# Cosine attention and an MLP mixer on one core: a new order of the end phase, with one product of the weights on GpSimd

## The chip, the cores and the metric

One core of a Trainium2 chip runs the whole program. The metric is the time of one execution in device microseconds; the time before is the median of three runs. The engines are named as in the profile: PE is TensorE's matmul, PEld its weight load, DVE is VectorE, ACT is ScalarE, POOL is GpSimd, SP is SyncE, which issues most DMAs.

## The reference

For 8 batches, 12 heads, 448 positions and heads of 64, attention on normalised rows is followed by a mixer over positions and one over channels:

```python
q_n = q / (np.linalg.norm(q, axis=-1, keepdims=True) + 1e-06)
k_n = k / (np.linalg.norm(k, axis=-1, keepdims=True) + 1e-06)
scores = np.matmul(q_n, k_n.transpose(0, 1, 3, 2)) / tau
attn = softmax(scores)                      # over the last axis
x = (attn @ v), heads side by side          # (8, 448, 768)
h = np.maximum(x.transpose(0, 2, 1) @ w_tok1, 0.0) @ w_tok2     # 448 -> 256 -> 448
u = x + h.transpose(0, 2, 1)
out = u + np.maximum(u @ w_ch1, 0.0) @ w_ch2                    # 768 -> 1536 -> 768
```

## The kernel before, in words

The loop runs over 48 pairs of heads, six to a batch. Each pair is loaded, normalised, transposed, scored, put through the exponential, multiplied by v, and mixed over positions (`tok1`, `tok2`); the result `u` of a batch is transposed into `ut`. The two products of the channel mixer for batches 0 to 5 are cut into units and fed into TensorE's stream beside the attention of later batches. Everything is written out by hand under `manual_schedule`: each engine executes its instructions in the order in which the code names them, and an instruction waits only for the data and buffers that it needs.

The last two batches (B0 and B1, numbers 6 and 7) have no later attention to lie beside. They are computed in an **end phase** (from line 959) that saves matmuls: each of the two channel products is split into 2 x 2 blocks and done with seven half-size products in place of eight, from sums and differences of blocks (Winograd's form of Strassen's method).

*First layer* (`p1` to `p7`, lines 595 to 626). The weights' sums are s1w, s2w, s3 (written in place into `wc1t`) and s4w, made by `fast_weights1`, line 547; the inputs' differences t1x to t4x are made by `fast_x`, line 561. `p1(d)` to `p7(d)` run for d = 0, 1, 2, a third of the hidden channels each; each is one product of 12 matmuls with 448 columns. PSUM banks X, Y and Z are taken in turn from a pool of three (`ps2`). A product that adds onto a bank (`start` is False: p2 on X, p3 on Z, p7 and p4 on Y) waits until the engine that copied out the bank's earlier state is done. The partial results go into SBUF copies: e1 (ScalarE, after p1), e5 (ScalarE, after p5), e16 (VectorE, after p6) and e167 (VectorE, after p7). e16 and e167 have two buffers each, e5 has one. The hidden tile `gt` has four quarters for each d: ScalarE writes the first from p2 with its relu; VectorE adds p3 and e16, then ScalarE takes the relu; VectorE adds p4 and e1; and GpSimd adds e167 and e5 (`c22`, line 616). The relu of the last two, which are the second half of the hidden channels in B0 and in B1, is one operation over both batches (`relus`, line 628).

*Second layer* (`q1` to `q7`, lines 681 to 723). The seven row tiles of 128 rows are tiles 0 to 2 in B0, 4 to 6 in B1, and tile 3, the **shared** tile, with the last 64 rows of B0 and the first 64 of B1. Six form three groups of two (`TILES`, line 644), and each group goes through q1 to q7, 6 matmuls of 384 columns each. The weights' differences t1w to t4w are made by `fast_weights2` (line 635), the differences of the hidden tile s1g to s4g for each group by `fast_g` (line 650, VectorE). Here too q2 adds onto q1's bank (psXo), q3 onto q5's (psZo), q7 and q4 onto q6's (psYo). ScalarE copies q1 to f1 and q5 to f5; VectorE makes f16 and f167 from psYo and f1; VectorE and GpSimd add these to the rows `orow`, which SP stores (`store_row`). The shared tile is multiplied plainly in three column ranges (0 to 384, 384 to 640, 640 to 768; `shared_part`, `shared_out`, `shared_store`). Its first range stands between q1 and the groups, the other two at the end.

The order of the end phase is the list of calls from line 959 to 1045. In it t4x is one GpSimd operation and s4w one VectorE operation (lines 986 and 987), GpSimd then runs t1w, c22(0), t2w, c22(1), c22(2), and the loop of the second layer is:

```python
for g in range(3):
    if g == 2:
        q1(g)
    if g == 0:
        q2(g)
        fast_g(0, 4)
    q5(g)
    q6(g)
    if g == 0:
        fast_weights2(4, nc.vector)
    for n, q in enumerate((q2, q7, q3, q4)):
        if g or n:
            q(g)
        if g < 2:
            fast_g(g + 1, n + 1)
```

Of the kernel before, what the change touches and what calls it, by code (L numbers as in the profile page):

```python
# [7 lines left out]
FP32 = mybir.dt.float32  # L8
FP16 = mybir.dt.float16
AF = mybir.ActivationFunctionType  # L10
# [12 lines left out]
def kernel(  # L23
# [12 lines left out]
    nc = tc.nc  # L36
# [510 lines left out]
    def fast_weights1(n, eng):  # L547
        s, w = fw["s"], w1part
        out, a, b, op = {1: (s[0], w(1, 0), w(1, 1), ALU.add), 2: (s[1], s[0], w(0, 0), ALU.subtract),
                         3: (w(1, 0), w(0, 0), w(1, 0), ALU.subtract), 4: (s[2], w(0, 1), s[1], ALU.subtract)}[n]  # L550
        tt(eng, out if n == 3 else out[:], a[:] if n == 2 else a, b[:] if n == 4 else b, op)
# [9 lines left out]
    def fast_x(k, j0, j1, eng=None):  # L561
        t = fw["t"]
        a, b = {1: (cols(B1, j0, j1), cols(B0, j0, j1)),
                2: (cols(B1, HD + j0, HD + j1), t[1][:, j0:j1]),
                3: (cols(B1, HD + j0, HD + j1), cols(B1, j0, j1)),
                4: (cols(B0, HD + j0, HD + j1), t[2][:, j0:j1])}[k]
        tt(eng or nc.vector, t[k][:, j0:j1], a, b, ALU.subtract)
# [8 lines left out]
    def bank2(kind, d):  # L576
        t = ps2.tile([128, 2, 512], FP32, name=f"ps{kind}_{d}", tag="s")
        {"X": px, "Y": py, "Z": pz}[kind][d] = t
# [9 lines left out]
    def etile(kind, d, bufs=1):  # L588
        e[kind, d] = (tail if kind == "e1" and d == 0 else tail2).tile([128, 2, S], FP32, name=f"{kind}_{d}", tag=kind, bufs=bufs)
        return e[kind, d][:]  # L590
# [12 lines left out]

    def p5(d):
        prod1(5, d, pz, True)
        nc.scalar.activation(out=etile("e5", d), in_=pz[d][:, :, 0:S], func=AF.Copy)

    def p6(d):
        prod1(6, d, py, True)
# [2 lines left out]
    def p7(d):  # L612
        prod1(7, d, py, False)
        tt(nc.vector, etile("e167", d, 2), py[d][:, :, 0:S], e["e1", d][:], ALU.add)

    def c22(d):
        tt(nc.gpsimd, gpart(1, 1, d), e["e167", d][:], e["e5", d][:], ALU.add)

    def p3(d):
        prod1(3, d, pz, False)  # L620
        tt(nc.vector, gpart(0, 1, d), pz[d][:, :, 0:S], e["e16", d][:], ALU.add)
        nc.scalar.activation(out=gpart(0, 1, d), in_=gpart(0, 1, d), func=AF.Relu)

    def p4(d):
        prod1(4, d, py, False)
        tt(nc.vector, gpart(1, 0, d), py[d][:, :, 0:S], e["e1", d][:], ALU.add)

    def relus(d):
        g = gts[B0 // 2][:, HC + 2 * d:HC + 2 * d + 2, :]
        if d == 1:  # L630
            nc.scalar.activation(out=g, in_=g, func=AF.Relu)
        else:
            nc.vector.tensor_scalar_max(out=g, in0=g, scalar1=0.0)

    def fast_weights2(n, eng):
        def w(i, j):
            return wc2t[:, HC * i:HC * (i + 1), DH * j:DH * (j + 1)]

        t = fw["t2"]
        a, b = {1: (w(0, 1), w(0, 0)), 2: (w(1, 1), t[1][:]), 3: (w(1, 1), w(0, 1)), 4: (w(1, 0), t[2][:])}[n]  # L640
        tt(eng, t[n][:], a, b, ALU.subtract)
        fw[2] = {1: w(0, 0), 2: w(1, 0), 3: w(1, 1), 4: t[4], 5: t[1], 6: t[2], 7: t[3]}

    TILES = ((0, 1), (4, 5), (2, 6))
    sg, xo, yo, zo, eo, orow = {}, {}, {}, {}, {}, {}

    def gtile(t, i, j0=0, j1=HC):
# [26 lines left out]
        b, slot = (B0, t) if t < 3 else (B1, t - 3)  # L674
        return u16[b][:, HD * h:HD * (h + 1), slot]

    def etile2(kind, g, bufs=1):
        eo[kind, g] = tail2.tile([128, DH], FP32, name=f"{kind}_{g}", tag=kind, bufs=bufs)
        return eo[kind, g][:]

    def q1(g):
        xo[g] = ps.tile([128, 512], FP32, name=f"psXo_{g}", tag="b")
        prod2(1, g, xo[g][:, 0:DH], True)
        nc.scalar.activation(out=etile2("f1", g, 2), in_=xo[g][:, 0:DH], func=AF.Copy)
        tt(nc.gpsimd, j3(etile2("f1u", g, 2)), j3(eo["f1", g][:]), urow(TILES[g][1], 0), ALU.add)

# [35 lines left out]
        tt(nc.vector, orow[g][1][:, 0:DH], yo[g][:, 0:DH], eo["f1u", g][:], ALU.add)  # L722
        store_row(TILES[g][1], orow[g][1])

    def shared_part(lo, hi, j0, j1):
        if j0 == 0:
            shared[lo] = (ps if lo else ps2).tile([128, 512], FP32, name=f"psF_shared_{lo}", tag="b" if lo else "s")
        psF = shared[lo]
        for j in range(j0, j1):
            for i in range(2):  # L730
                nc.tensor.matmul(psF[:, 0:hi - lo], gts[B0 // 2][:, HC * i + j, 384:512], wc2t[:, HC * i + j, lo:hi],
                                 start=(i + j == 0), stop=(i == 1 and j == HC - 1))

    def shared_out(lo, hi):
        o, psF = shared["o"], shared[lo]
        for r, b, slot in ((0, B0, 3), (64, B1, 0)):
            nc.vector.tensor_tensor(out=j3(o[r:r + 64, lo:hi]), in0=j3(psF[r:r + 64, 0:hi - lo]),
                                    in1=u16[b][r:r + 64, lo // 128:hi // 128, slot], op=ALU.add)
# [27 lines left out]
    with tc.manual_schedule():  # L766
# [142 lines left out]
        for i in range(NPAIR + 1, NP_ALL):  # L909
            b, pj = i // NPAIR, i % NPAIR  # L910
            for c in range(KC):
                score(i, c)
            if i == NPAIR + 1:
                upose(i - 4, 2)
                tok2(i - 2, pe=True)
                pv_wide(i - 1)
                upose_act(i - 2)
                x_wide(i - 1)
                sums(i + 2)
            else:  # L920
                pv_rest(i - 1)
                pv(i - 1, 0)
                pv(i - 1, 1)
            if i == NP_ALL - 1:
                fast_weights1(2, nc.vector)
            if i == NPAIR + 1:
                refill(0)
            elif pj == 2 and 1 < b < B - 1:
                refill(b - 1)
            side(i)  # L930
            if i == NP_ALL - NPAIR:
                fed[1] = (sum(t for t, _ in queue) - fed[0]) / NPAIR
            fed[0] += fed[1]
            unit(True)
            if old(i):
                score(i, KC)
            else:
                score_rest(i)
            if i > NPAIR + 1:
                tok2(i - 2)  # L940
            if i + 1 < DMA_T0:
                tpose(i + 1)
            if due():
                unit(True)
            while due():
                unit()
            tok1(i - 1)
            if i + 3 < NP_ALL:
                sums(i + 3)
            if i == NP_ALL - 3:  # L950
                early.close()
                tail = ctx.enter_context(tc.tile_pool(name="tail", bufs=1, side="right", reuse_waits="tile"))
                tail_tiles()
            if i == NP_ALL - 2:
                fast_weights1(1, nc.gpsimd)
        last = NP_ALL - 1
        while queue:
            unit(True)
# [10 lines left out]
        p2(0)  # L969
        tok2(last - 1, pe=True)  # L970
        tok1(last)
        fast_x(2, 0, 1)
        fast_x(3, 0, 1)
        p2(1)
        upose(last - 1)
        fast_x(2, 1, 2)
        fast_x(3, 1, 2)
        p1(2)
        tok2(last, pe=True)
        bank2("Z", 0)  # L980
# [1 line left out]
        upose(last)  # L982
        p2(2)
        fast_x(2, 2, 3)
        fast_x(3, 2, 3)
        fast_x(4, 0, HD, nc.gpsimd)
        fast_weights1(4, nc.vector)
        fast_weights2(1, nc.gpsimd)
        bank2("Y", 0)
        p6(0)  # L990
        bank2("Y", 1)
# [2 lines left out]
        p7(0)  # L994
        c22(0)
        p7(1)
        fast_weights2(2, nc.gpsimd)
        bank2("Y", 2)
        p6(2)
        p4(0)  # L1000
        p4(1)
        p7(2)
        fast_weights2(3, nc.vector)
        bank2("Z", 1)
        p5(1)
        c22(1)
        bank2("Z", 2)
        p5(2)
        c22(2)
        relus(1)  # L1010
        p4(2)
        p3(1)
        p3(2)
        q1(0)
        relus(0)
        q1(1)
        relus(2)
        shared_part(0, DH, 0, 4)
        fast_g(0, 1)
        shared_part(0, DH, 4, HC)  # L1020
        fast_g(0, 2)
        fast_g(0, 3)
        shared_out(0, DH)
        for g in range(3):
            if g == 2:
                q1(g)
            if g == 0:
                q2(g)
                fast_g(0, 4)
            q5(g)  # L1030
            q6(g)
            if g == 0:
                fast_weights2(4, nc.vector)
            for n, q in enumerate((q2, q7, q3, q4)):
                if g or n:
                    q(g)
                if g < 2:
                    fast_g(g + 1, n + 1)
        for lo, hi in ((DH, D - 128), (D - 128, D)):
            shared_part(lo, hi, 0, HC)  # L1040
            shared_out(lo, hi)
            if lo == DH:
                shared_store(0, hi, (nc.sync, nc.sync))
            else:
                shared_store(lo, hi, (nc.scalar, nc.sync))


# [33 lines left out]
```

## Time and profile before

| what | value |
|---|---|
| median of 3 runs | 388.77 us (387.48 to 388.85) |
| profiled execution, its whole time | 387.23 us |
| its span, from the first to the last instruction | 385.4 us |
| mean granted TensorE clock | 0.995 |
| first product of the end phase, p1(0), starts | 322.32 us |
| first product of the second layer, q1(0), starts | 353.58 us |
| last shared matmuls start | 378.63 us |

Times inside the profile count from the start of the span. A line of the timeline has the start, the time taken, the engine, the line of the kernel, the operation, what it writes and reads with the shapes, how many instructions are merged in it, and in brackets the idle time of the engine just before it and what ended that. The times of matmuls overlap each other by a little, so the pace of a stream is read from start to start. Tiles have the code's names: `e` stands for e1, e5, e16 and e167, `f` for the copies of the second layer, `gt` for the hidden tile.

### The profile page before, as it was taken

What the parts mean: (1) busy time and instruction counts of PE and PEld (TensorE: products, weight loads), DVE (VectorE), ACT (ScalarE), POOL (GpSimd) and SP (SyncE); (2) the same over time, 40 slices, a digit from 0 to 9 for tenths busy, and PEclk for the clock granted to TensorE, in tenths of its full rate; (3) what the DMA queues carried; (4) which work ended last, traced back from release to release, by engine and by line L of the source; (5) the groups of instructions that cost most, each with busy time, mean ns of one, the idle gap of its engine ahead of it and who ended that gap; (6) DMA issues with size and microseconds to landing.
All of it is one profiled execution on the core that took longest, in us unless ns stands there. A gap on an engine that the chain in (4) does not pass through costs nothing.

```text
span 385.4 us, 10254 instructions
## 1 busy us (share of the span) xinstructions
PE 366.6 (95%) x4086; PEld 239.7 (62%) x4086; DVE 253.9 (66%) x563; ACT 230.7 (60%) x395; POOL 276.7 (72%) x403
## 2 busy tenths in 40 slices
PE   7798999999999999999999999999999999896895
PEld 6466666776566666676566666666657766453463
DVE  7789766776346665466437565456437768897973
ACT  6899887855676458746666457746667645415010
POOL 8999988979666586677667587677667880497642
PEclk9899999999999999999999999999999999999999
DMA  7999999989978788879767978868866664000054
GB/s 201 268 245 210 261 247 193 212 163 180 210 182 166 193 178 204 202 134 217 205 148 149 231 158 215 186 139 207 211 153 134 149 126 108 0 0 1 2 162 126
DMA packets 115936, 64.35 MB, mean 167 GB/s; under 512 B 72240, under 2 KB 112304, under 8 KB 115888
## 3 DMA queue, kind: packets, MB, share of 16 engines
q1 hardware_dynamic: 109936, 58.22, 67.0%
q0 software_dynamic: 5616, 5.21, 8.8%
q8 instruction: 32, 0.52, 0.6%
q10 hardware_dynamic: 336, 0.26, 0.2%
q14 instruction: 16, 0.13, 0.1%
HBM read 43.45 MB, written 11.01 MB: 141 GB/s over the span
## 4 chain that ended last, share of the span: by engine, by line
PE 75%; POOL 7%; issue 6%; ACT 5%; DVE 4%; DMA 2%; ACTq 0%; DVEq 0%; POOLq 0%
PE psG L466 21%; PE psF L482 19%; PE psO L383 9%; PE psS L344 8%; PE psU L433 5%; PE psR L419 5%; ACT pt L345 3%; PE psYo L667 2%; PE psQ L351 2%; POOL t1w L536 1%; PE psZo L667 1%; POOL s1w L536 1%; PE psXo L667 1%; PE psO L366 1%; DVE ssq L265 1%
## 5 line engine op out<-in xcount | busy, mean ns | idle before, releaser
L345 ACT ACTIVATE pt<-psS 128x896 f16<-128x896 f32 (+1 forms) x156 | 132.4, 917 | 52.9 <-PE psS L344 52.7
L297 POOL TENSOR_TENSOR kq<-kf,rn 128x384 f16<-128x384 f32 (+1 forms) x47 | 41.9, 891 | 66.7 <-DVE rn L274 62.9
L482 PE MATMUL psF<-wc2t,gt 128*128 128x384 f16 x504 | 88.4, 326 | 0.0
L466 PE MATMUL psG<-ut,wc1t 128*128 128x448 f16 x432 | 88.1, 352 | 0.0
L482 PEld LDWEIGHTS <-gt 128*128 128x128 f16 x504 | 47.1, 98 | 27.8
L466 PEld LDWEIGHTS <-wc1t 128*128 128x128 f16 x432 | 40.2, 98 | 32.4
L469 ACT ACTIVATE gt<-psG 128x448 f16<-128x448 f32 x72 | 38.9, 540 | 33.1 <-PE psG L466 33.1
L265 DVE TENSOR_REDUCE ssq<-sq 128x15 f32<-128x960 f32 (+2 forms) x51 | 56.1, 1100 | 3.3 <-ACT sq L247 3.0
L422 DVE TENSOR_SCALAR rt<-psR 128x256 f16<-128x256 f32 x48 | 20.0, 417 | 50.8 <-PE psR L419 50.8
L297 POOL TENSOR_TENSOR kq<-qf,rn 112x512 f16<-112x512 f32 x45 | 47.1, 1046 | 3.0
L344 PE MATMUL psS<-qk 64*128 64x448 f16 x312 | 41.4, 356 | 3.6 <-DVE qk L323 2.9
L486 DVE TENSOR_TENSOR ost<-psF,u 128x384 f32<-128x384 f32 (+1 forms) x48 | 25.6, 534 | 24.3 <-PE psF L482 22.9
L249 POOL TENSOR_TENSOR sq<-qf 112x512 f32<-112x512 f32 x39 | 40.6, 1042 | 0.0
L249 POOL TENSOR_TENSOR sq<-kf 128x384 f32<-128x384 f32 (+1 forms) x46 | 40.2, 874 | 0.1
L383 PE MATMUL psO<-vt,pt 128*128 128x65 f16 (+1 forms) x1024 | 39.1, 193 | 0.0
L387 DVE TENSOR_TENSOR x<-psO,rec 128x256 f16<-128x256 f32 x82 | 34.8, 424 | 2.8
L383 PEld LDWEIGHTS <-pt 128*128 128x128 f16 (+1 forms) x1024 | 34.2, 97 | 3.5 <-issue 0.9
L436 DVE TENSOR_TENSOR u<-psU,x 128x512 f16<-128x512 f32 x48 | 32.3, 674 | 2.1 <-PE psU L433 0.6
L419 PEld LDWEIGHTS <-w1t 128*128 128x128 f16 x384 | 24.8, 98 | 7.9 <-issue 2.1
L419 PE MATMUL psR<-x,w1t 128*128 128x128 f16 x384 | 29.3, 219 | 0.2 <-DVE u L436 0.2
L433 PEld LDWEIGHTS <-w2t 128*128 128x128 f16 x384 | 24.8, 98 | 7.5 <-issue 1.0
L433 PE MATMUL psU<-rt,w2t 128*128 128x128 f16 x384 | 29.3, 219 | 0.0
(117 smaller groups left out, 474.4 us busy)
## 6 DMA issues: line engine op xcount, KB each, us to landing
qf<-in_q_dram SPq DMA_DIRECT2D x47, 224.0 KB, 4.1
kf<-in_k_dram SPq DMA_DIRECT2D x36, 192.0 KB, 3.8
vf<-in_v_dram SPq DMA_DIRECT2D x36, 192.0 KB, 3.8
vf<-in_v_dram SPq DMA_DIRECT2D x12, 224.0 KB, 8.0
kf<-in_k_dram SPq DMA_DIRECT2D x11, 224.0 KB, 8.8
wc1t<-in_moe_w_ch_dram POOLq DMA_DIRECT2D x4, 576.0 KB, 10.2
wc2t<-in_moe_w_ch_dram POOLq DMA_DIRECT2D x2, 1152.0 KB, 12.3
out_dram<-ost SPq DMA_DIRECT2D x6, 336.0 KB, 3.6
```

What stands on the lines that cost most here:

```text
L249: nc.gpsimd.tensor_mul(out=dst, in0=src, in1=src)
L265: nc.vector.tensor_reduce(out=st["ssq"][0:n, sl], in_=st["sq"][0:n, sl], axis=AXX.X, op=ALU.add)
L297: eng.tensor_tensor(out=kq[0:p, a, 0:n].rearrange("p c g e -> p g c e"), in0=st["kq"[a]][:].rearrange("p (g c) e -> p g c e", g=2), in1=_b ...
L344: nc.tensor.matmul(psS[:, hh, 0:S], qk[hb, c * n:c * n + 128], qm[hb], start=True, stop=True)
L345: nc.scalar.activation(out=pts[i % 2][0:n, 2 * S * c:2 * S * (c + 1)].rearrange("p (h s) -> p h s", h=2), in_=psS[0:n, :, 0:S], func=AF.Ex ...
L383: nc.tensor.matmul(psO[:, m, 0:E + 1], pts[i % 2][0:n, at:at + 128], vt[0:n, i % HP, nch * hh + c, 0:E + 1], start=(old(i) and c == 0), st ...
L387: nc.vector.tensor_tensor(out=st["x"][:, :, hh * E:(hh + 1) * E], in0=psO[:, :, 0:E], in1=_bcast_free(rec[:], E), op=ALU.mult)
L419: nc.tensor.matmul(psR[:, tt], w1t[:, w1[m], tt * 128:(tt + 1) * 128], st["x"][:, m], start=(m == 0), stop=(m == 3))
L433: nc.tensor.matmul(psU[:, m], w2t[:, tt, lo:lo + 128], st["rt"][:, tt], start=(tt == 0), stop=(tt == TT - 1))
L466: nc.tensor.matmul(psG[:, 0:S], wc1t[:, dt, ct * 128:(ct + 1) * 128], ut[b][:, dt].rearrange("p m s -> p (m s)")[:, lo:lo + S], start=(dt ...
L469: nc.scalar.activation(out=gt[:, ct, (b % 2) * S:(b % 2 + 1) * S], in_=psG[:, 0:S], func=AF.Relu)
L482: nc.tensor.matmul(psF[:, 0:hi - lo], gt[:, ct, at:at + 128], wc2t[:, ct, lo:hi], start=(ct == 0), stop=(ct == CT - 1))
```

## The change

The reordering touches the end phase alone.

- In the first layer, e5 gets a second buffer. s4w moves from VectorE in the end phase to GpSimd in the last pass of the main loop. t4x is cut: its first two pieces go to VectorE, right after t2x and t3x, and only the third stays on GpSimd.
- On GpSimd, t2w moves ahead of c22(0).
- The relu over both batches becomes `relu21` (VectorE, B0) and `relu22` (ScalarE, B1), each by d and each placed behind the addition that it belongs to.
- The groups become (0, 1), (2, 6), (4, 5). The differences of group 0 and q1 start before the last additions of p3.
- Each group runs q5, q2, q6, q7, q3, q4. `f5`, `f16` and `f167` use the two-buffered places of `e5`, `e16` and `e167`.
- The shared tile is computed wholly after the groups, and its stores go out in three ranges.

```diff
     def p5(d):
         prod1(5, d, pz, True)
-        nc.scalar.activation(out=etile("e5", d), in_=pz[d][:, :, 0:S], func=AF.Copy)
+        nc.scalar.activation(out=etile("e5", d, 2), in_=pz[d][:, :, 0:S], func=AF.Copy)
...
-    def relus(d):
-        g = gts[B0 // 2][:, HC + 2 * d:HC + 2 * d + 2, :]
-        if d == 1:
-            nc.scalar.activation(out=g, in_=g, func=AF.Relu)
-        else:
-            nc.vector.tensor_scalar_max(out=g, in0=g, scalar1=0.0)
+    def relu21(d):
+        nc.vector.tensor_scalar_max(out=gpart(1, 0, d), in0=gpart(1, 0, d), scalar1=0.0)
+
+    def relu22(d):
+        nc.scalar.activation(out=gpart(1, 1, d), in_=gpart(1, 1, d), func=AF.Relu)
...
-    TILES = ((0, 1), (4, 5), (2, 6))
+    TILES = ((0, 1), (2, 6), (4, 5))
...
-    def etile2(kind, g, bufs=1):
-        eo[kind, g] = tail2.tile([128, DH], FP32, name=f"{kind}_{g}", tag=kind, bufs=bufs)
+    def etile2(kind, g, bufs=2):
+        eo[kind, g] = tail2.tile([128, DH], FP32, name=f"{kind}_{g}", tag=kind.replace("f", "e") if kind in ("f5", "f16", "f167") else kind, bufs=bufs)
...
-    def shared_part(lo, hi, j0, j1):
-        if j0 == 0:
-            shared[lo] = (ps if lo else ps2).tile([128, 512], FP32, name=f"psF_shared_{lo}", tag="b" if lo else "s")
+    def shared_unit(lo, hi):
+        shared[lo] = ps.tile([128, 512], FP32, name=f"psF_shared_{lo}", tag="b")
         psF = shared[lo]
-        for j in range(j0, j1):
+        for j in range(HC):
...
             if i == NP_ALL - 2:
                 fast_weights1(1, nc.gpsimd)
+            if i == NP_ALL - 1:
+                fast_weights1(4, nc.gpsimd)
...
         tok1(last)
-        fast_x(2, 0, 1)
-        fast_x(3, 0, 1)
+        for k in (2, 3, 4):
+            fast_x(k, 0, 1)
         p2(1)
         upose(last - 1)
-        fast_x(2, 1, 2)
-        fast_x(3, 1, 2)
+        for k in (2, 3, 4):
+            fast_x(k, 1, 2)
...
         fast_x(2, 2, 3)
+        fast_x(4, 2, 3, nc.gpsimd)
         fast_x(3, 2, 3)
-        fast_x(4, 0, HD, nc.gpsimd)
-        fast_weights1(4, nc.vector)
         fast_weights2(1, nc.gpsimd)
+        fast_weights2(2, nc.gpsimd)
...
         p7(1)
-        fast_weights2(2, nc.gpsimd)
         bank2("Y", 2)
         p6(2)
         p4(0)
+        relu21(0)
         p4(1)
         p7(2)
+        relu21(1)
         fast_weights2(3, nc.vector)
         bank2("Z", 1)
         p5(1)
         c22(1)
         bank2("Z", 2)
         p5(2)
+        relu22(0)
         c22(2)
-        relus(1)
         p4(2)
+        relu21(2)
+        fast_g(0, 1)
         p3(1)
+        fast_g(0, 2)
         p3(2)
+        relu22(1)
         q1(0)
-        relus(0)
         q1(1)
-        relus(2)
-        shared_part(0, DH, 0, 4)
-        fast_g(0, 1)
-        shared_part(0, DH, 4, HC)
-        fast_g(0, 2)
+        relu22(2)
+        q5(0)
+        q2(0)
         fast_g(0, 3)
-        shared_out(0, DH)
-        for g in range(3):
...
+        q6(0)
+        fast_g(0, 4)
+        fast_weights2(4, nc.vector)
+        for n, q in enumerate((q7, q3, q4)):
+            q(0)
+            fast_g(1, n + 1)
+        fast_g(1, 4)
+        for g in (1, 2):
             if g == 2:
                 q1(g)
...
+            for n, q in enumerate((q5, q2, q6, q7, q3, q4)):
+                q(g)
+                if g == 1 and n < 4:
+                    fast_g(2, n + 1)
-        for lo, hi in ((DH, D - 128), (D - 128, D)):
-            shared_part(lo, hi, 0, HC)
+        for lo, hi in ((0, DH), (DH, D - 128), (D - 128, D)):
+            shared_unit(lo, hi)
             shared_out(lo, hi)
-            if lo == DH:
-                shared_store(0, hi, (nc.sync, nc.sync))
-            else:
-                shared_store(lo, hi, (nc.scalar, nc.sync))
+            shared_store(lo, hi, (nc.scalar if hi == D else nc.sync, nc.sync))
```

More of the change, by code (lines that the diff above doesn't have):

```diff
@@ L1008 @@
         p5(2)
+        relu22(0)
         c22(2)
-        relus(1)
         p4(2)
+        relu21(2)
+        fast_g(0, 1)
         p3(1)
+        fast_g(0, 2)
         p3(2)
+        relu22(1)
         q1(0)
-        relus(0)
         q1(1)
-        relus(2)
-        shared_part(0, DH, 0, 4)
-        fast_g(0, 1)
-        shared_part(0, DH, 4, HC)
-        fast_g(0, 2)
-        fast_g(0, 3)
-        shared_out(0, DH)
-        for g in range(3):
+        relu22(2)
+        q5(0)
+        q2(0)
+        fast_g(0, 3)
+        q6(0)
[6 more added lines that the diff above has]
+        for g in (1, 2):
             if g == 2:
                 q1(g)
[L1027 to L1038, printed above, removed]
-        for lo, hi in ((DH, D - 128), (D - 128, D)):
-            shared_part(lo, hi, 0, HC)
+            for n, q in enumerate((q5, q2, q6, q7, q3, q4)):
[4 more added lines that the diff above has]
+            shared_unit(lo, hi)
             shared_out(lo, hi)
-            if lo == DH:
-                shared_store(0, hi, (nc.sync, nc.sync))
-            else:
-                shared_store(lo, hi, (nc.scalar, nc.sync))
+            shared_store(lo, hi, (nc.scalar if hi == D else nc.sync, nc.sync))
 _INS = ['q', 'k', 'v', 'tau', 'moe_w_tok1', 'moe_w_tok2', 'moe_w_ch1', 'moe_w_ch2']
```

## The prediction

> **What bounds the kernel now.** I read the page first, then TensorE's own waits, then the timeline of each engine over the end phase (322 us to the end of the span). The page says that TensorE is the engine to watch:
>
> ```profile
> span 385.4 us, 10254 instructions
> PE 366.6 (95%) x4086; PEld 239.7 (62%) x4086; DVE 253.9 (66%) x563; ACT 230.7 (60%) x395; POOL 276.7 (72%) x403
> ```
>
> So a change of the end phase is worth what it does to TensorE's stops there, and to the tail behind the last matmul. Its waits from 330 to 381 us (engine, tile, what it waited for: us in total, times, longest):
>
> ```profile
> PE psZ L585 <- ACT e L606: 2.4, 1, 2.4
> PE psZ L585 <- DVE s4w L536: 1.6, 1, 1.6
> PE psYo L667 <- DVE f L536: 1.5, 2, 0.8
> PE psXo L667 <- ACT gt L622: 0.6, 1, 0.6
> ```
>
> I price each stop as the delay of a start against TensorE's pace. The timeline gives the pace: one product of the first layer takes 1.135 us (two from 338.51 to 340.78), one of the second 0.975 (thirteen from 365.95 to 378.63), twelve shared matmuls of 384 columns 1.95 (356.31 to 358.26). By it p3(0) starts 1.81 late (337.37, due 335.56), p3(2) 2.59, q1(1) ends 0.78 late, q7(0) starts 0.88 late and q4(0) 0.97: **7.0 us of stops**. The two that teach most are these:
>
> ```profile
> 352.45 1.29 PE L585 MATMUL psZ<-ut,s4w 128*128 128x448 f16 x6 [2.43 <-ACT e L606]
> ...
> 360.21 1.14 PE L667 MATMUL psYo<-t2w,s2g 128*128 128x384 f16 x6
> 362.06 1.14 PE L667 MATMUL psYo<-t3w,s3g 128*128 128x384 f16 x6 [0.72 <-DVE f L536]
> ```
>
> The first is the lone e5 buffer: e5(2) is copied only when c22(1) has read e5(1). The second is structural: q7 adds onto q6's bank, so it must wait until VectorE has copied q6 out. Wherever q7 directly follows q6, the stop is about 0.85 us (0.25 to VectorE's start, 0.56 copy, 0.05 back).
>
> **The port between VectorE and GpSimd** decides the rest. VectorE and GpSimd lines:
>
> ```profile
> 320.23 1.35 DVE L536 TENSOR_TENSOR s2w<-s1w,wc1t 128x2304 f16<-128x2304 f16 x1
> ...
> 333.43 3.88 DVE L536 TENSOR_TENSOR s4w<-wc1t,s2w 128x2304 f16<-128x2304 f16 x1
> ...
> 346.60 2.91 DVE L536 TENSOR_TENSOR t3w<-wc2t 128x2304 f16<-128x2304 f16 x1
> ```
> ```profile
> 333.29 2.80 POOL L536 TENSOR_TENSOR t4x<-ut,t2x 128x1344 f16<-128x1344 f16 x1 [15.31 <-DVE t2x L536]
> 336.06 5.68 POOL L536 TENSOR_TENSOR t1w<-wc2t 128x2304 f16<-128x2304 f16 x1
> ...
> 343.73 4.57 POOL L536 TENSOR_TENSOR t2w<-wc2t,t1w 128x2304 f16<-128x2304 f16 x1
> 348.24 3.21 POOL L536 TENSOR_TENSOR gt<-e,e 128x896 f16<-128x896 f32 x1
> ```
>
> The same 2304 elements take VectorE 1.35 us with GpSimd idle, and 3.88 or 2.91 beside it. s4w ends (337.31) 1.2 us after t4x ends (336.09); t3w ends 1.3 after t2w (348.24). In turn t1w and the c22 at 348.24 lose 1.1 us until s4w and t3w are through. So an f16 VectorE operation between SBUF tiles and a GpSimd operation exclude each other, whoever waits goes next, and they alternate. VectorE reads of PSUM run beside GpSimd unhindered (two e copies in 2.08 us during t1w). Alone, t1w and t2w need 4.5 us and a c22 2.07.
>
> **The change, part by part**, with the built program's order on each engine.
>
> *S4 to GpSimd, t4x to VectorE for two of three pieces.* GpSimd idles 15.3 us before t4x, so s4w fits: it starts when s2w is done (321.66) and ends at 326.16. Cost: s3 (wc1t, 325.63) waits for the port, 0.53; two t4x pieces of 0.30 follow. VectorE's u of the last pair starts at 331.4 instead of 331.0, and the last upose 0.22 late. p3(0) starts at 335.78, without the 1.81. Unseen is s4w beside VectorE at that place: 4.5 to 5.7 us (the two lengths of t1w and t2w); I take 4.5, since VectorE's work there reads PSUM. At 5.7, TensorE starts 1.2 later.
> The Trainium skill, Perfetto Trace Analysis, section Optimizing Scalar/DVE Operations, warns that moving work between VectorE and GpSimd might not help because they share a port. By that rule alone this part would be worth nothing; the rows say the waiting shrinks from 1.81 to 0.22, as the GpSimd stretch was empty.
>
> *Order of GpSimd.* t4x(2) 333.7 to 334.6, t1w to 339.1, t2w to 343.65, and only then c22(0), which ran ahead of t2w before (341.68).
>
> *Second e5 buffer.* p3(2) no longer waits for e5(2): the 2.59 goes. Late next is e167(2): its two buffers are unchanged, so it waits for c22(0). On VectorE, relu21(0) is ready at 342.7, meets t2w, runs 343.65 to 343.95; gt of p4(1) ends 345.0 (p5(2) needs its bank: stop 0.25). c22(0) runs 343.97 to 346.03, so e167(2) 346.1 to 347.15, and p4(2) starts at 347.2, due 346.23: stop 0.97. Queued behind e167(2) on VectorE are relu21(1), t3w, gt of p4(2) and everything after; TensorE's p4(2), and through t3w and s1g the whole second layer, wait for them.
>
> *The relus apart.* Half of a 1792 relu (two in 1.15 us) is 0.3 each. Next: c22(1) 346.05 to 348.1, relu21(1) to 348.4, c22(2) to 350.45, t3w to 351.75, gt p4(2) to 352.72, relu21(2) to 353.05, s1g 353.66, gt p3(1) 354.57, s2g 355.05, gt p3(2) 356.14 (before: 354.93). No row shows whether a relu (one SBUF input) needs the port: not at all, or like the tensor_tensor rows. I take the second, its nearest rows.
> The Trainium skill, SBUF — State Buffer, section Who interferes with whom, says that tensor_scalar can run in a two-port mode and then blocks and is blocked for the whole instruction; by it the relus wait, which this trace neither shows nor excludes.
>
> *Group 0.* q1(1) reads a tile of the first batch, so its 0.78 goes. q5(0) is due at 352.55 and waits for s1g: 353.7, stop 1.15. q2(0) adds onto q1(0)'s bank and waits for ScalarE's f1(0), which now stands behind relu of p3(2) *and* relu22(1). From 356.17: 0.85 + 0.85 + 0.47 (pace and length in the timeline) give 358.35; q2(0) starts at 358.4, due 354.7: **stop 3.7**. Before, shared matmuls (1.95 us) covered this place; they now stand at the end, so no cover is left.
> Then q7(0) 0.85 as before; t4w waits for GpSimd's f16 sum (to 363.7), f167 follows, and q4(0) stops 1.1 (before 0.97).
>
> *Order q5, q2, q6, q7.* In groups 1 and 2, q2 stood between q6 and q7 and hid the copy. Now the 0.85 stop comes in both. In group 1 VectorE also has s1g, orow of q2 and s2g ahead of f16: six 0.47 steps from 366.37 put f16 at 369.2 and q7(1) at 369.8, due 368.15: 1.65.
>
> *Row copies with two buffers* (f5, f16, f167): TensorE never waited for these buffers, 0. *Shared row last*: same matmuls. Its stores come in three pieces, and the rows' stores leave 1.9 us earlier relative to the last matmul. The last store now lands 2.7 to 2.9 us after issue with 1152 KB around it; the shortest landing of any store in the end is 2.5. Gain 0 to 0.4; I take 0.2.
>
> **Sum.** After: 0.22 + 0.25 + 0.97 + 1.15 + 3.7 + 0.85 + 1.1 + 1.65 + 0.85 = 10.7 us of stops against 7.0, less 0.2: **+3.5 us**. The profiled execution took 387.23 us (span 385.4, 1.8 around it), 1.5 under the median 388.77; I add the difference to the median: **392.3 us**.
>
> **Rivals.**
> 1. *Relus need no port.* t3w then precedes c22(2), gt p3(2) ends 1.67 earlier: +1.8, 390.6. For: one input. Against: the f16 rows above. Chance 0.14.
> 2. *VectorE keeps the port between relu21(1) and t3w*: 1.05 earlier, 391.2. Against: at 356.7 to 359 s2g and s3g alternate with GpSimd's f1u. Chance 0.14.
> 3. *The other side: the port does not hold these operations* (c22 reads f32, not f16 as t1w did). Then gt p3(2) ends at 352.3, the q2(0) stop is 1.7, p4(2) 0.6, q4(0) 0.3, q7 0.85, 0.8, 0.85; 5.1 against 7.0, less 0.2: -2.1, 386.7. It decides once q2(0) starts before about 354.9. For: nothing but the type; against: the 3.21 of c22. Chance 0.16.
> 4. *GpSimd runs at its hindered lengths* (t2w 5.7, s4w 5.7): +1.1 to +2.5 more, 393.4 to 394.8. Chance 0.10.
>
> The forecast has 0.46. About 0.5% (1.9 us) is what a measurement of this kernel can tell from no change. Faster by more: the lower part of rival 3, 0.10. Within: the rest of it 0.06, 0.10 of rival 1, 0.04 of rival 2, 0.03 of the forecast: 0.23. Slower: 0.67. The range runs from 388.0 (leaving most of rival 3, 0.14) to 394.0 (leaving 0.06 of rival 4).
>
> **What the profile after would show.** Right: no wait of psZ for s4w or for e; s3 stretched beyond 1.8 us; e167(2) starting as c22(0) ends; a TensorE wait of 3 to 4 us of psXo for ScalarE's f at q2(0); three psYo waits of 0.6 to 1.5 for f16, one in each group; the last matmul near 384.4. Wrong: t3w at 1.35 us beside a c22, or f1 ready when q5(0) ends. Then the q2(0) stop, a third of the sum, is gone.

## The result, and the profile after

The changed kernel takes 392.85 us (median of six runs, 391.25 to 393.67) against 388.79 us of the kernel before on the same chip: a ratio of 1.0101, 95% interval 1.0073 to 1.013. It is slower. The profiled execution took 392.43 us, with a mean granted clock of 0.991.

The page of the kernel after, its span and the busy time of each engine:

```profile
span 390.6 us, 10263 instructions
...
PE 367.0 (94%) x4086; PEld 238.7 (61%) x4086; DVE 251.8 (64%) x565; ACT 231.1 (59%) x397; POOL 276.6 (71%) x404
```

The span grew by 5.2 us and TensorE's busy time over the whole by 0.4, but this small number hides two that nearly cancel. From p1(0) to the end of the span TensorE's busy time grew by 2.57 us (52.30 to 54.87) and its idle time by 2.21; ahead of p1(0) its busy time fell by 2.22 (there the profile before has a stretch of 3.4 us at half clock, from 12.9 to 16.3 us, and the one after none). So in the end phase some of what was added is waiting, and some is slower matmuls. TensorE's waits of the kernel after, 330 to 386 us (tile, what it waited for: us in total, times, longest):

```profile
PE psXo L666 <- ACT f L683: 3.5, 1, 3.5
PE psYo L666 <- DVE f L536: 3.4, 4, 1.2
PE psZo L666 <- DVE s1g L536: 1.1, 1, 1.1
PE psY L585 <- DVE e L536: 0.8, 1, 0.8
```

Both waits of psZ, for s4w and for e, are gone. In their place stand one of 3.5 us for ScalarE's copy f1, one for s1g, one for e167 and two more for f16. TensorE's timeline of the kernel after, where each of them ends:

```profile
347.49 1.29 PE L585 MATMUL psY<-t4x,wc1t 128*128 128x448 f16 x6 [0.78 <-DVE e L536]
...
354.06 1.15 PE L666 MATMUL psZo<-t1w,s1g 128*128 128x384 f16 x6 [1.06 <-DVE s1g L536]
358.73 2.08 PE L666 MATMUL psXo<-wc2t,gt 128*128 128x384 f16 x6 [3.51 <-ACT f L683]
360.60 2.12 PE L666 MATMUL psYo<-t2w,s2g 128*128 128x384 f16 x6
...
371.61 1.14 PE L666 MATMUL psYo<-t3w,s3g 128*128 128x384 f16 x6 [1.20 <-DVE f L536]
```

In order these are p4(2), q5(0), q2(0), q6(0) and q7(1). Look at the second column too: q2(0) took 1.87 us from start to start instead of 0.975, and q6(0) 2.12 us from its first matmul to the end of its last, where the others take 1.14. Their clock was halved (the windows at the end of this text show it), which the sum did not have. (A product of the first layer is six matmuls of 448 columns, as the x6 of its rows says, and not the 12 named ahead of the prediction; the pace of 1.135 us was read from rows and holds.)

ScalarE's timeline of the kernel after shows why f1 was late:

```profile
355.04 0.95 ACT L622 ACTIVATE gt<-gt 128x896 f16<-128x896 f16 x1 [6.48 <-DVE gt L536]
356.51 0.95 ACT L622 ACTIVATE gt<-gt 128x896 f16<-128x896 f16 x1 [0.52 <-DVE gt L536]
357.37 0.93 ACT L632 ACTIVATE gt<-gt 128x896 f16<-128x896 f16 x1
358.20 0.85 ACT L683 ACTIVATE f<-psXo 128x384 f32<-128x384 f32 x2
```

The relus of p3(1) and p3(2) and relu22(1) stand ahead of f1(0), which is the first of the two copies merged in the last line. The bank that f1(0) reads had been full since about 352. For most of the time since, ScalarE was not busy: it stood idle for 6.48 us until VectorE's addition for p3(1) was there, and 0.52 more for that of p3(2). A ready copy waited behind relus whose inputs were late.

VectorE's timeline of the kernel after shows the port:

```profile
343.15 1.21 DVE L629 TENSOR_SCALAR gt<-gt 128x896 f16<-128x896 f16 x1
...
346.34 1.09 DVE L536 TENSOR_TENSOR e<-psY,e 128x896 f32<-128x896 f32 x1 [0.98 <-POOL gt L536]
347.35 1.41 DVE L629 TENSOR_SCALAR gt<-gt 128x896 f16<-128x896 f16 x1
348.68 3.23 DVE L536 TENSOR_TENSOR t3w<-wc2t 128x2304 f16<-128x2304 f16 x1
...
352.95 0.39 DVE L629 TENSOR_SCALAR gt<-gt 128x896 f16<-128x896 f16 x1
```

The same relu takes 0.39 us with GpSimd idle, and 1.21 and 1.41 beside its operations (t2w and the addition c22(1)); t3w takes 3.23 against the 1.35 of the same form alone.

### The profile page after: what moved, and what is told of

It is laid out like the page before. It is cut to its first block, busy times and chain, and to the rows that moved or that the text cites. A ratio compares the mean times of both kernels' runs of the same rounds, so it can differ in the third digit from the quotient of the medians.

```text
span 390.6 us, 10263 instructions
## 1 busy us (share of the span) xinstructions
PE 367.0 (94%) x4086; PEld 238.7 (61%) x4086; DVE 251.8 (64%) x565; ACT 231.1 (59%) x397; POOL 276.6 (71%) x404
## 4 chain that ended last, share of the span: by engine, by line
PE 78%; DVE 6%; POOL 5%; DMA 4%; issue 3%; ACT 2%; SPq 0%; DVEq 0%; ACTq 0%; POOLq 0%
PE psG L466 20%; PE psF L482 19%; PE psO L383 9%; PE psS L344 7%; PE psU L433 5%; PE psR L419 5%; DMA qk<-kq 2%; POOL kq L297 2%; PE psYo L666 2%; PE psX L585 2%; PE psQ L351 2%; DMA qf<-in_q_dram 1%; PE psO L366 1%; PE psY L585 1%; PE psXo L666 1%
```

## The experiments

Each kernel ran beside the kernel before on the same chip, and the median of the kernel before differs a little from chip to chip (387.8 to 388.8 us where it is quoted here); kernels of different chips are compared by their ratios. A profile is of one execution, and the stages ahead of the end phase shift it by up to 3 us (p1(0) starts anywhere from 322.1 to 325.1). So beside the ratio stands the **stretch**: from the start of p1(0) to that of the last 24 shared matmuls (ranges two and three), with 1.95 us added for the kernels in which the first twelve come last too. It holds the same work in every kernel, but for the matmuls that two of them have in addition.

| kernel | median, us | ratio to before (95%) | stretch, us |
|---|---|---|---|
| before | 388.79 | | 56.31 |
| after | 392.85 | 1.0101 (1.0073 to 1.013) | 61.43 |
| f1 ahead of the relus | 387.77 | 1.0001 (0.9976 to 1.0027) | 56.91 |
| added matmuls in the stop | 392.06 | 1.0091 (1.0066 to 1.0115) | 59.54 |
| order q5, q6, q2, q7 | 391.12 | 1.0080 (1.0055 to 1.0104) | 60.34 |
| the first and the third together | 386.02 | 0.9946 (0.9925 to 0.9967) | 55.25 |
| the same, relu21 on ScalarE | 383.29 | 0.9872 (0.9849 to 0.9894) | 52.83 |
| c22(0) ahead of t2w | 391.06 | 1.0061 (1.0037 to 1.0084) | 59.66 |
| before, s4w on GpSimd | 385.82 | 0.9934 (0.9914 to 0.9955) | 54.40 |
| before, two buffers | 389.18 | 1.0006 (0.9980 to 1.0033) | 56.94 |
| before, both | 384.17 | 0.9882 (0.9863 to 0.9902) | 53.00 |
| before, two buffers, added matmuls | 386.86 | 0.9965 (0.9952 to 0.9979) | 55.27 |
| before, both and the new groups | 383.60 | 0.9881 (0.9849 to 0.9912) | 51.71 |

### Is the stop at q2(0) ScalarE's queue?

From the kernel after; on ScalarE the relus of p3(1) and p3(2) and relu22(1) go behind f1(0) and f1(1), ahead of relu22(2).

```diff
-        p3(1)
+        p3(1, False)
         fast_g(0, 2)
-        p3(2)
-        relu22(1)
+        p3(2, False)
         q1(0)
         q1(1)
+        relu12(1)
+        relu12(2)
+        relu22(1)
         relu22(2)
```

> The changed kernel with one reordering on ScalarE: f1(0) and f1(1) are copied ahead of the relus of p3(1), p3(2), relu22(1) and relu22(2). Theory (the q2(0) stop is the queue of relus ahead of f1 on ScalarE, and the halved TensorE clock is a consequence of that idle time): the 3.7 us wait of psXo for f falls below 0.3, no stretch at half clock in the end phase, q2(0) and q6(0) take 0.98 us each instead of 1.87; in all 5.0 to 5.5 us less than the changed kernel, about 387.5 us, just under the kernel before. Rival (VectorE's backlog is the limit, and the stop only moves to its next copy): f16(0) or f167(0) makes TensorE wait 2 us and more, and the time falls by less than 2 us.

The ratio is 1.0001 against 1.0101 of the kernel after, 1.0% less, and the stretch 4.5 us less, somewhat under the 5.0 to 5.5 expected. The wait for f1 is gone, and so is the half clock in the end phase. Two prices came back. GpSimd's f1u (the sum of f1 and u), released earlier, now stands beside relu21(2) and s1g, and TensorE waits longer for s1g. The timelines of this kernel, TensorE's, GpSimd's and VectorE's:

```profile
354.87 1.15 PE L670 MATMUL psZo<-t1w,s1g 128*128 128x384 f16 x6 [2.03 <-DVE s1g L536]
```
```profile
352.48 1.93 POOL L536 TENSOR_TENSOR f1u<-f,u 128x384 f32<-128x384 f32 x2 [1.92 <-ACT f L687]
```
```profile
353.74 1.08 DVE L536 TENSOR_TENSOR s1g<-gt 128x768 f16<-128x768 f16 x1
```

s1g took 1.08 us instead of 0.56, relu21(2) 0.83 instead of 0.39, and the wait at q5(0) went from 1.06 to 2.03. And f5 now comes behind the relus on ScalarE, which stops q3(0) for 0.50. A queue that was shortened in one place started another engine sooner, and here that one collided.

### Is the slow q2(0) the clock?

From the kernel after; 62 matmuls of 128 columns are added where TensorE waits for f1(0). They write unused columns of a PSUM bank and feed no output.

```diff
         q5(0)
+        for _ in range(62):
+            nc.tensor.matmul(yo[0][:, 384:512], id16[:], id16[:], start=True, stop=True, skip_group_check=True)
         q2(0)
```

> The changed kernel with 62 idle matmuls of 128 columns, into unused columns of a bank, put between q5(0) and q2(0), so that TensorE has about 3.5 us to do while it would wait for f1(0). They add no result. Theory (the clock is halved because TensorE stood still for 3.5 us): the wait for f1 stays in the chain, but the clock stays at 1.0 and q2(0) and q6(0) take 0.98 us each: 1.8 us less than the changed kernel in the profile, about 390.6 us, and less spread between runs. Rival (the half clock comes from elsewhere, such as the time since the start): still 6.8 us at half clock, and no gain or up to 0.5 us of loss.

TensorE's timeline of this kernel:

```profile
360.94 1.14 PE L666 MATMUL psXo<-wc2t,gt 128*128 128x384 f16 x6
361.91 1.14 PE L666 MATMUL psYo<-t2w,s2g 128*128 128x384 f16 x6
```

q2(0) started at 360.94 and q6(0) at 361.91, 0.975 apart; the clock stayed full in the end phase, and the stretch shrank by 1.89 us, the size of the slow matmuls (1.85). So the stop itself still costs 3.7, and the clock behind it was a second price. The whole time does not show it: 392.06 us where 390.6 was expected, a ratio of 1.0091 against 1.0101 with overlapping intervals. The profiled execution also had 10.2 us of half clock near its start; for the others no trace says where the time went.

### The stops at q7

From the kernel after; groups 1 and 2 run q6 ahead of q2.

```diff
-            for n, q in enumerate((q5, q2, q6, q7, q3, q4)):
+            for n, q in enumerate((q5, q6, q2, q7, q3, q4)):
```

> The changed kernel with groups 1 and 2 in the order q5, q6, q2, q7, q3, q4, so that q2 stands between q6 and q7 again. Theory (q7 behind q6 exposes the copy f16): the psYo stop of group 2 (0.88) goes, that of group 1 (1.36) falls to 0.4 or less, in all 1.8 to 2.2 us less than the changed kernel, about 390.8 us. Rival (VectorE's differences s1g and s2g for the next group stand ahead of f16, and the order of the products does not matter): group 1 keeps 1 us or more, and the gain is under 1 us.

The stops of 1.36 and 0.88 at q7(1) and q7(2) are gone. The stretch gives 1.1 of these 2.2 us, since in this execution the half clock lasted 10.2 us instead of 6.8, over q7(0), q3(0) and part of q4(0) as well. By the time alone the rival would stand: 391.12 us, a gain of 0.2% with overlapping intervals, is the gain of under 1 us that it named. The trace is against it, since group 1 kept no stop.

The two edits together, f1 ahead and q6 ahead of q2:

> The changed kernel with both edits: f1 ahead of the relus on ScalarE, and q2 between q6 and q7 in groups 1 and 2. Theory: the gains add, 5.2 and 2.0 us, so about 385.5 us, 0.7 to 1.0% faster than the kernel before. Rival (with the f1 stop gone VectorE has no slack left in groups 0 and 1, and its queue takes over as the bound): the sum falls short by 2 us or more, 387.5 us or slower.

A ratio of 0.9946, 1.55% less than the kernel after, where the two alone gave 1.00% and 0.21%; by the stretch 6.2 us against 4.5 and 1.1. It is a little more than the sum, and the trace has a reason: no half clock lies in this end phase, so the order q5, q6, q2, q7 takes 1.66 us off here (56.91 to 55.25) against 1.1 alone. Of the 2.24 us of stops at q7(1) and q7(2), 0.37 is left at q7(1), where VectorE's copy f16 still comes late; the rest of the difference is smaller waits.

### Is the port between VectorE and GpSimd part of it?

From the last kernel; relu21 moves from VectorE to ScalarE, whose relu of this shape took 0.94 us beside GpSimd's additions and 0.93 without (in the kernel after, at 347.62 and 357.37).

```diff
-        nc.vector.tensor_scalar_max(out=gpart(1, 0, d), in0=gpart(1, 0, d), scalar1=0.0)
+        nc.scalar.activation(out=gpart(1, 0, d), in_=gpart(1, 0, d), func=AF.Relu)
```

> The changed kernel with f1 ahead of the relus, q2 between q6 and q7, and relu21 on ScalarE in place of VectorE. Theory (relu21 takes part in the exclusion between VectorE and GpSimd, and by alternating it lets c22(2) in ahead of t3w): without it t3w goes between c22(1) and c22(2) and ends near 349.8 us instead of 351.8, the wait of psZo for s1g (2.0 us) falls below 0.3, and the time is 1.7 to 2.2 us less than with the two edits alone, about 384.0 us. Rival (the wait for s1g comes from GpSimd's c22 alone, the relu takes no part): t3w still ends after 351 us, and the gain is under 0.5 us.

VectorE's timeline of this kernel:

```profile
346.98 2.54 DVE L536 TENSOR_TENSOR t3w<-wc2t 128x2304 f16<-128x2304 f16 x1
...
351.54 0.56 DVE L536 TENSOR_TENSOR s1g<-gt 128x768 f16<-128x768 f16 x1 [1.01 <-ACT gt L633]
```

t3w ends at 349.5, 2.4 us ahead of the kernel after; s1g is done before q5(0) asks for it, and the wait of 2.03 is gone. The ratio fell from 0.9946 to 0.9872: this version, at 383.29 us, beats both kernels. So VectorE's relus did need the port: the edit also takes work off VectorE, but the one relu between e167(2) and t3w is 0.39 us of work with GpSimd idle, and t3w came 2.4 us sooner. An edit from the other side shows it again: from the kernel after, t2w goes back behind c22(0) on GpSimd.

```diff
         fast_weights2(1, nc.gpsimd)
-        fast_weights2(2, nc.gpsimd)
...
         p7(1)
+        fast_weights2(2, nc.gpsimd)
```

> The changed kernel with c22(0) ahead of t2w on GpSimd again. Theory (relu21(0) can't run while t2w does, so the wait moves from e167(2) to the relu): relu21(0) ends near 346.7 us, p5(2) starts 2.6 us late instead of 0.2, e167(2) no longer waits for c22(0), and the time is within 1 us of the changed kernel, or up to 2 us less if TensorE's idle time before q2(0) falls to 3 us and the clock is not halved. Rival (the relu runs beside GpSimd): p5(2) is not late, the 0.9 us stop of p4(2) goes, and the gain is 1 us or more with the clock halved as before.

GpSimd's and VectorE's timelines of this kernel:

```profile
341.24 4.54 POOL L536 TENSOR_TENSOR t2w<-wc2t,t1w 128x2304 f16<-128x2304 f16 x1
```
```profile
342.49 3.54 DVE L629 TENSOR_SCALAR gt<-gt 128x896 f16<-128x896 f16 x1
```

relu21(0) is blocked for the rest of t2w and takes 3.54 us. Behind it in VectorE's queue the addition of p4(1) comes late, TensorE stops 2.35 us at p5(2), and the half clock follows there. The wait at p4(2) goes, the one at q2(0) shrinks to 1.80, and the whole is 391.06 us. So the place of t2w behind c22(0), which the kernel before had, brings little once the relus stand apart (1.0061 against 1.0101, overlapping intervals).

The Trainium skill, SBUF — State Buffer, section SBUF: two separate sides, says that the shared port pair is an exclusive lock, held for a whole instruction, and that the other side fully blocks. The relu rows (0.39 free; 1.21, 1.41 and 3.54 beside GpSimd) agree.

### The parts alone, from the kernel before

s4w on GpSimd, t4x cut; nothing else:

```diff
+            if i == NP_ALL - 1:
+                fast_weights1(4, nc.gpsimd)
...
-        fast_x(2, 0, 1)
-        fast_x(3, 0, 1)
+        for k in (2, 3, 4):
+            fast_x(k, 0, 1)
...
-        fast_weights1(4, nc.vector)
```

> The kernel before with one part of the change: s4w on GpSimd in the main loop, t4x in three pieces of which two are on VectorE. Theory (GpSimd's stretch was empty, and the rest of its queue starts earlier with it): the stop of psZ for s4w (1.6 us) goes, upose comes up to 0.2 us late, t1w, c22(0), t2w and c22(1) end about 2 us earlier, and so does everything behind e5(2): 1.6 to 2.2 us less than the kernel before. Rival (the port is the limit, moving work between VectorE and GpSimd gives nothing): within 0.5 us of the kernel before.

GpSimd's timeline, and TensorE's first wait, of this kernel:

```profile
321.79 4.55 POOL L536 TENSOR_TENSOR s4w<-wc1t,s2w 128x2304 f16<-128x2304 f16 x1 [3.63 <-DVE s2w L536]
```
```profile
PE psZ L585 <- ACT e L606: 1.8, 1, 1.8
```

s4w fits into GpSimd's idle stretch at its unhindered length, p3(0) no longer waits, and the time is 0.66% under that of the kernel before. The wait of p3(2) for e shrank as well, from 2.4 to 1.8.

Two buffers alone:

```diff
-        nc.scalar.activation(out=etile("e5", d), in_=pz[d][:, :, 0:S], func=AF.Copy)
+        nc.scalar.activation(out=etile("e5", d, 2), in_=pz[d][:, :, 0:S], func=AF.Copy)
...
-    def etile2(kind, g, bufs=1):
+    def etile2(kind, g, bufs=2):
```

> The kernel before with one part of the change: two buffers for e5, and the row copies in the two-buffered places. Theory: the 2.4 us wait of psZ for e5 goes, but what follows is then held by GpSimd's c22(2) and VectorE's relus, so about 1.0 us less than the kernel before (0.8 to 1.4). Rivals: the whole 2.4 us, if nothing else is late; or nothing, if the relus of the third part were late anyway.

No gain (1.0006), though p3(2) no longer waits. TensorE's timeline of this kernel:

```profile
355.77 0.50 PE L667 MATMUL psXo<-wc2t,gt 128*128 128x384 f16 x2 [1.61 <-ACT gt L622]
356.61 0.65 PE L667 MATMUL psXo<-wc2t,gt 128*128 128x384 f16 x2 [0.34 <-ACT gt L622]
357.06 3.68 PE L731 MATMUL psF_shared<-wc2t,gt 128*128 128x384 f16 x12
```

The wait became another: q1(1) reaches the relus of p3 1.95 us early. And in that place the clock fell, so the twelve shared matmuls took 3.52 us from start to start instead of 1.95. To tell the two apart, 34 matmuls of 128 columns without any result of use were put into that wait:

```diff
         q1(0)
         relus(0)
+        xo[1] = ps.tile([128, 512], FP32, name="psXo_1", tag="b")
+        for _ in range(34):
+            nc.tensor.matmul(xo[1][:, 384:512], id16[:], id16[:], start=True, stop=True, skip_group_check=True)
         q1(1)
```

> The kernel before with two buffers for each partial copy, and 34 matmuls of 128 columns without any result of use, in unused columns of a PSUM bank, where TensorE waits ahead of q1(1); they are added work and feed no output. Theory (the half clock behind that wait ate what the second buffer gained): no half clock in the end phase, the twelve shared matmuls take 1.95 us and not 3.52, p3(2)'s wait stays gone, and the time is 385.5 to 387 us, ratio about 0.994. Rival (the second buffer gains nothing by itself, the wait only moves on to the relu): the time stays near 389 us, ratio about 1.000, with the clock full in the end phase.

TensorE's timeline of this kernel:

```profile
353.60 2.06 PE L1019 MATMUL psXo<-id 128*128 128x128 f16 x34
...
356.89 2.11 PE L732 MATMUL psF_shared<-wc2t,gt 128*128 128x384 f16 x12
358.84 1.14 PE L667 MATMUL psXo<-wc2t,gt 128*128 128x384 f16 x6
```

The twelve take 1.95 us again, the stretch is 1.67 shorter, and the time is 386.86 us, at the top of what the theory gave (385.5 to 387), with a ratio of 0.9965 against the 0.994 named. Added matmuls made the kernel faster. Without the half clock the second buffer gains 0.35% (1.0 us by the stretch); the half clock had taken all of it.

Both parts together, on the kernel before:

> The kernel before with two parts of the change together: s4w and t4x as in the change, and two buffers for each partial copy; order of the calls, relus, groups and shared tile as before. Theory (stops add up by the stream's pace): beside the first part alone (385.82 us) p3(2)'s wait for e5 (1.8 us there) goes, p3(2) ends earlier and q1(1) then waits some 2 us for the relu of p3(2), so about 1.4 us less than the first part alone: 384.4 us, ratio to the kernel before about 0.989. Rival (a wait of 2 us in front of the second layer lets the clock fall, as in the run with two buffers alone): the last stretch shows a half clock of 3.4 us or more beside that wait, and the time is 386 us or above, no better than the first part alone.

384.17 us, a ratio of 0.9882; the theory said 384.4 and 0.989. The waits in front of the second layer are 1.01 and 0.34 us, and the clock did not fall in the end phase. That the second buffer is worth 1.4 us by the stretch here and nothing alone is this difference.

Then with the groups as in the change, since q1(1) reads a tile of the first batch in that order:

```diff
-    TILES = ((0, 1), (4, 5), (2, 6))
+    TILES = ((0, 1), (2, 6), (4, 5))
```

> The kernel before with three parts of the change: s4w and t4x, two buffers for each partial copy, and the groups of row tiles in the order (0, 1), (2, 6), (4, 5); the order of the calls, the relus and the shared tile as before. Theory: q1(1) then reads tile 2, which does not need p3(2), so its two stops (1.01 and 0.34 us with the first two parts alone) go; the first shared matmuls reach the chunks that need the relu of p3(2) at about 355.35, as it ends: 1.3 us less than the first two parts alone, 382.9 us, ratio to the kernel before about 0.985. Rival: the wait only moves on into the shared matmuls, or f1(1) and what follows on ScalarE comes late for q2(0), and the time stays at 384 us or above, ratio 0.988 or more.

TensorE's timeline of this kernel:

```profile
350.60 2.11 PE L667 MATMUL psXo<-wc2t,gt 128*128 128x384 f16 x12
352.55 0.33 PE L731 MATMUL psF_shared<-wc2t,gt 128*128 128x384 f16 x1
353.14 1.95 PE L731 MATMUL psF_shared<-wc2t,gt 128*128 128x384 f16 x11 [0.27 <-DVE gt L633]
```

q1(1) runs through, and 0.27 us of the wait moved into the shared matmuls. The stretch is 1.29 us shorter, as the theory had it (1.3). The times do not show it: 383.60 us, a ratio of 0.9881 (0.9849 to 0.9912) against 0.9882 without it, and the theory's 0.985 lies at the edge of the interval. So it is seen in one trace and not in the medians.

## Why the prediction was right, point by point

The forecast was 3.5 us more, 392.3 us; the medians moved by 4.06, to 392.85. Its stops against those of the profile after, priced in the same way:

| step | predicted | measured |
|---|---|---|
| p3(0), from upose (transposing u) | 0.22 | 0.12 |
| p5(2), gt of p4(1) | 0.25 | 0.19 |
| p4(2), e167(2) behind c22(0) | 0.97 | 0.93 |
| q5(0), s1g | 1.15 | 1.22 |
| q2(0), f1(0) | 3.70 | 3.70 |
| q2(0), q6(0) at half clock | none | 1.85 |
| q7(0) | 0.85 | 0.90 |
| q4(0) | 1.10 | 0.97 |
| q7(1) | 1.65 | 1.36 |
| q7(2) | 0.85 | 0.88 |
| sum, against 7.0 before | 10.7 | 12.1 |

- **What was right.** Every stop came where it was put, and none of the nine differs by over 0.3 us. s4w at 4.55 and t2w at 4.56 us were the unhindered lengths that the prediction chose; s3 stretched to 1.79 (the sign named was beyond 1.8); c22(0) ended at 346.31 and e167(2) started at 346.34.
- **What failed.** The step "one of the second 0.975" was used as the pace of every product. Behind the stop of 3.7 us two products ran at half clock. The kernels with f1 ahead and with added matmuls both show it gone with full clock. This term of 1.85 us is larger than all other errors of the sum together. One of the signs named for the profile after was missed with it: the last matmul was to end near 384.4 us and ended at 386.43.
- **Smaller ones.** p1(0) started 0.44 us later than in the profile before, ahead of the end phase; the tail shrank by 0.36 instead of 0.2 (the stores of the shared row landed 1.9 to 2.2 us after issue). 12.1 - 7.0 + 0.44 - 0.36 is the 5.2 by which the spans differ.
- **Profile and medians.** The profiled executions differ by 5.2 us, the medians by 4.06: the profile before lay 1.56 us under its median, the one after 0.42 under its own. Against the profiles the sum is 1.7 us short (387.23 + 3.5 is 390.7, against 392.43). That the forecast came within 0.55 us of the median is thus partly luck: adding the stops to the median hid most of the missing term. The mean clock of each execution is on record, and the times of the kernel after follow it (391.25 to 392.43 us at 0.991, 393.27 to 393.67 at 0.986); where in the kernel it fell, only the profiled ones show.
- **The rivals.** *Relus need no port*: out, by 1.21, 1.41 and 3.54 against 0.39 us. *VectorE keeps the port*: out, t3w took 3.23 and ended 1.2 us behind c22(2). *The port does not hold these operations*: out, by the same rows: q2(0) started at 358.73, not before 354.9, and relu21 on ScalarE took 0.74% off. *Hindered lengths on GpSimd*: out, 4.55 and 4.56.
- **Where the gain went.** s4w on GpSimd, two buffers and the new groups by themselves take 4.6 us off the stretch of the kernel before. The order written with them puts 9.7 on again (61.43 against 51.71): f1 behind relus and the clock behind that (4.5 with f1 ahead), relu21 on VectorE (2.4), and q7 directly behind q6 (1.7). These three are steps taken one after another, and another order could divide them otherwise. What is left, 1.1, was not taken apart. Among the stops left in the fastest kernel built on the one after is the 0.80 at p4(2).

## What to carry to other kernels

Price a copy that frees a PSUM bank by everything queued ahead of it on its engine: f1 was ready to run at about 352 and ran at 358.2, behind three relus that nothing needed yet, and for most of that time ScalarE stood idle for the input of the first. When the last of them got its input (4.5 us after f1 was ready) counted for more than how long they took from there (1.7). When a change bundles several edits, cost each alone on the kernel before: here three that gain 1.2% together were buried under an order that lost more. And a stop on TensorE can cost a second time, in the clock of what follows (after stops of 1.95, 2.35 and 3.5 us here, but not after one of 2.03), so the pace in a sum holds only while nothing long stands before it.

## What the runs showed of the hardware

The granted clock fell to half and rose again in steps of about 3.41 us: the half-clock stretches inside the work lasted 3.4, 6.8 or 10.2 us in every trace. Laid on that grid, windows of the kernel after (stretch, length, then busy time and instructions of PE, PEld, DVE, ACT and POOL, then granted clock, DMA share, GB/s):

```profile
352.61:356.02 3.41, 1.54 (x9) 0.61 (x8) 3.27 (x6) 0.95 (x1) 0.00 (x0) 1.00 0.00 0
356.02:359.43 3.41, 0.70 (x3) 0.36 (x3) 0.46 (x1) 2.92 (x5) 0.68 (x1) 0.50 0.00 0
359.43:362.85 3.42, 3.29 (x11) 1.36 (x10) 1.05 (x3) 0.84 (x2) 1.10 (x2) 0.50 0.00 0
362.85:366.26 3.41, 2.11 (x12) 1.17 (x12) 3.41 (x5) 0.00 (x0) 2.80 (x2) 1.00 0.00 0
```

The windows of the kernel with q6 ahead of q2, and one of the kernel with f1 ahead:

```profile
357.08:360.49 3.41, 2.20 (x8) 1.02 (x8) 0.09 (x1) 2.76 (x5) 1.78 (x2) 0.50 0.00 0
360.49:363.90 3.41, 2.70 (x9) 1.15 (x8) 2.46 (x5) 0.00 (x0) 0.88 (x1) 0.50 0.00 0
363.90:367.32 3.42, 3.42 (x12) 1.62 (x11) 2.90 (x4) 0.00 (x0) 3.34 (x3) 0.50 0.00 0
```
```profile
351.30:354.71 3.41, 1.55 (x10) 0.70 (x8) 3.27 (x4) 0.98 (x2) 1.86 (x2) 1.00 0.00 0
```

The clock fell after a window with 1.54 us of TensorE work in it, and rose after one with 3.29. With 2.20 and 2.70 us it did not rise, which is why the half clock lasted a window longer there. With 1.55 us in the last row it did not fall, against 1.54 in the first. In the end phases of all kernels here no window with more than 1.54 us lost the clock, and none with less than 1.55 kept it. Over whole executions it is no edge in busy time, though. Two windows of the kernel before, one near its start and one in the end phase, and one near the start of the kernel with two buffers alone:

```profile
9.49:12.90 3.41, 1.85 (x20) 0.95 (x20) 2.83 (x7) 3.41 (x6) 3.34 (x4) 1.00 1.18 262
350.82:354.24 3.42, 1.79 (x11) 0.97 (x11) 1.09 (x2) 2.76 (x3) 2.39 (x2) 1.00 0.00 0
```
```profile
12.08:15.49 3.41, 3.29 (x23) 1.58 (x24) 2.72 (x7) 2.41 (x6) 2.72 (x4) 0.50 1.17 266
```

The clock fell behind the first, with 1.85 us, and held behind the second, with 1.79; it stayed at half behind the third, with the same 3.29 us behind which it rose above. So the profile's busy time alone does not decide, and what does stays open. Stops of like size cost differently: one of 2.03 us nothing more with f1 ahead, 1.95 us in two parts 1.6 more with two buffers alone; the stop of 3.7 us cost 1.85 more in the kernel after, and with q6 ahead of q2 about 3 (five products took 4.0 us longer and covered the 0.97 of the stop at q4(0)). Where the grid lies against the stop would account for this, but no run moved the grid alone. The times of the kernel with two buffers alone fit it: its twelve runs spread from 385.47 us (mean clock 0.999) to 390.31 (0.982).

The Trainium skill, TensorE: Matmul & The Clock Gate, section What's actually happening, states a free-running window of 3413 ns, half clock after an idle window and full clock after a busy one. The length agrees with the steps here. The rows differ in that the window did not have to be idle: 1.54 us of work in it was not enough to keep the clock.
